# Scatters queued behind the next masks, ranks in another buffer, even rows on VectorE, and a tail in another order

## The chip, the cores and the metric

The kernel runs on one core of one Trainium2 chip. The metric is the device time of one launch in microseconds. Each core has TensorE (matmuls, PE in the profile; PEld are its weight loads), VectorE (DVE), ScalarE (ACT), GpSimd (POOL) and SyncE (SP, which here only issues DMAs).

## The reference

Three layers, one behind the other, over 4 x 768 = 3072 tokens of 8 heads x 48 = 384 values, all in float32.

```
state = alpha_t * state + k_t v_t^T ;  y_t = q_t state           # linear attention with decay
e = argmax(x @ w_gate) ; p = softmax(...)[e] ; s = sigmoid(x @ w_output_gate)[e]
x2 = p * s * (relu(x @ w1[e]) @ w2[e])                            # top-1 of 8 experts, F = 1024
out = relu(x2 @ w_in)**2 @ w_out                                  # dense, F = 2048
```

## The kernel before

**Attention loop.** The tokens are cut into 24 chunks of 128 (six to a batch entry). All matrix work of a chunk is done on TensorE with several chunks in flight: iteration i of the loop (line 783) does scores(i+1), scaled(i+2) (k and q turned, and multiplied with the decay), rows(i-1) and logits(i-1) (attention output back to one row per token, and the gate logits), decay(i+3) (two scans on VectorE), khat(i+1), outputs(i) and update(i+1) (the state). The order of these calls is the order in which each engine gets its instructions; each engine works its queue in that order and waits by semaphores.

- scores (328): 16 matmul instructions into two PSUM tiles `sc`; ScalarE copies them to `m`, and GpSimd cuts out the causal half of each with an affine_select (341), the "masks". For the last two chunks VectorE does both at once (346).
- outputs (389) writes PSUM tile `y`, and ScalarE copies it to `yt` (407). rows (418) multiplies `yt` into PSUM tile `fx`; ScalarE copies 384 columns of it to `xn` (433), and logits (435) sums the other columns on VectorE.
- The PSUM tiles `y`, `fx` and `ku` have one buffer each, `sc` two.

**Routing.** Chunks form groups of 6, 6, 6, 3, 1, 1, 1 (GROUPS). When a group's logits are there, route (448) puts some ten small VectorE operations (softmax, argmax, one-hot) on an agenda, and every call of pulse(n) in the loop issues n of them. One iteration later, settle (351) issues ranks (496), small matmuls that count for each token how many earlier tokens chose its expert, and place (519), which reads them (`rp`, 524); nine further small steps (placed, 527) give the index `idx` and the gate `g`. Then move(n) (566) scales up to n rows of the group by their gate (even chunks on ScalarE, 572, odd ones on VectorE, 570) and at once scatters each to the DRAM buffer `xs`, sorted by expert, with an indirect DMA that GpSimd issues (scatter, 142: a small memset and the DMA). `pace` is 1 for iterations below 18 and 3 from there; move stands at three places of an iteration.

**Early experts.** The expert with the most tokens of groups 0 to 2 is picked, and at the end of iteration 20 gather_early (680) issues two DMAs that read its first 256 tokens back from `xs` into `gx`; they wait for all scatters before them.

**Tail** (815 to 863). After the loop: the last outputs; turn_early (690) turns the gathered tokens on TensorE (`tx`), ScalarE and VectorE split them in a high and a low half (696, 697: lambdas that run(steps) calls); parts(3) (184) splits the weights of unit 3 (ScalarE cast 186, VectorE subtraction 187); the groups of one chunk are routed by route_one (577), placed by place_one (629: rank matmuls, then `rp` 634 and `idx` 636 on VectorE) and sent by send (639). psum (486) says which buffer a rank tile uses. Then up1 (719) and down1 (737) begin the experts, three matmuls for each product (`three`, 1353: high and low halves).

**Experts and dense layer** (995 to 1134). 64 units of expert weights, then 16 of the dense layer over 6 blocks of 512 tokens, a stream of matmuls beside which weights are loaded and split.

Of the kernel before, what the change touches and what calls it, by code (L numbers as in the profile page):

```python
# [27 lines left out]
def moe_block_kernel(ctx: ExitStack, tc: tile.TileContext, q, k, v, alpha, w_gate, w_ogate,  # L28
# [39 lines left out]
    with tc.manual_schedule():  # L68
# [115 lines left out]
        def parts(n, engine=nc.gpsimd):  # L184
            w, raw = unit_tile(n), raws.pop(n)
            nc.scalar.copy(w[:, 0::2, :], raw)  # L186
            engine.tensor_tensor(out=w[:, 1::2, :], in0=raw, in1=w[:, 0::2, :].bitcast(F32),  # L187
                                 op=ALU.subtract)
# [86 lines left out]
        def pulse(n=2):  # L275

            while agenda and n:
                if next(agenda[0], None) is None:
                    agenda.pop(0)
                else:  # L280
                    n -= 1

        def decay(i, mid=None):
            if i >= NCH:
                return
            ps = turned("al", i)
            al = al_t[i % 2]
            nc.scalar.copy(al[:, 0:PQ].rearrange("p (r t) -> p r t", r=NP)[:, :, 1:],
                           ps[:, :, 1:])
            s = a3.tile([P, 2, PQ], F32, tag="sp", name="sp", bufs=4)  # L290
            suf, pre = s[:, 0, :], s[:, 1, :]
            nc.vector.tensor_tensor_scan(suf[:, ::-1], al[:, 1:PQ + 1][:, ::-1],
                                         ends.rearrange("p c t -> p (c t)")[:, ::-1],
                                         initial=0.0, op0=ALU.mult, op1=ALU.add)
            pe = a3.tile([P, NP], F32, tag="pend", name="pend", bufs=4)
            nc.vector.tensor_tensor(out=pe, in0=ps[:, :, 0], in1=suf[:, 0:PQ:P], op=ALU.mult)
            pend[i] = pe
            pulse()
            sp[i] = s
            if mid:  # L300
                mid()
            d = d1_t[i % 2]
            nc.vector.reciprocal(d[:, 0:PQ:P], suf[:, 0:PQ:P])
            nc.vector.tensor_tensor_scan(pre, al[:, 0:PQ], d, initial=0.0, op0=ALU.mult,
                                         op1=ALU.add)
            pulse()

        def scaled(i, nms="kq"):
            if i >= NCH:
                return  # L310
            s = sp[i]
            for nm in nms:
                j, dst = (0, kh) if nm == "k" else (1, qh)
                ps = turned(nm, i)
                t = a3.tile([P, NP, P], F32, tag=nm + "h", name=nm + "h")
                nc.vector.tensor_tensor(out=t, in0=ps,
                                        in1=s[:, j, :].rearrange("p (r t) -> p r t", r=NP),
                                        op=ALU.mult)
                dst[i] = t
                pulse()  # L320
# [7 lines left out]
        def scores(i):  # L328
            if i >= NCH:
                return  # L330
            ps = [p_sc.tile([P, NP, P], F32, tag="sc", name="sc") for _ in range(2)]
            for pr in range(NP):
                for a in range(2):
                    r = slice(64 * a, 64 * a + D)
                    nc.tensor.matmul(ps[a][:, pr, :], kh[i][r, pr, :], qh[i][r, pr, :],  # L335
                                     start=True, stop=True)
            for a in range(2):
                m = ms_p.tile([P, NP, P], F32, tag="m", name="m")
                if i < NCH - 2:
                    nc.scalar.copy(m, ps[a])  # L340
                    nc.gpsimd.affine_select(out=m, in_=m, pattern=[[0, NP], [1, P]],
                                            compare_op=ALU.is_ge, fill=0.0, base=0,
                                            channel_multiplier=-1)
                else:

                    nc.vector.tensor_tensor(out=m, in0=ps[a],
                                            in1=mask.unsqueeze(1).to_broadcast([P, NP, P]),
                                            op=ALU.mult)
                msk[i, a] = m

        def settle(groups):
            for gi in groups:
                place(gi, ranks(gi))
# [14 lines left out]
        def update(i):  # L368
            if not has_next(i):
                return  # L370
            t = khn.pop(i)
            vt = slot("v", i)
            ps = p_1.tile([P, NP, D], F32, tag="ku", name="u")
            for pr in range(NP):
                for a in range(2):
                    nc.tensor.matmul(ps[64 * a:64 * a + 64, pr, :], t[:, pr, 64 * a:64 * a + 64],  # L376
                                     vt[:, 2 * pr + a, 0:D], start=True, stop=True)
            s = state[i % 3][:, :, 0:D]
            pb = pend[i + 1].unsqueeze(2).to_broadcast([P, NP, D])
            if i % NC == 0:  # L380
                nc.vector.tensor_tensor(out=s, in0=ps, in1=pb, op=ALU.mult)
            else:
                nc.vector.tensor_tensor(out=s, in0=ps, in1=st[i], op=ALU.add)
                pulse()
                nc.vector.tensor_tensor(out=s, in0=s, in1=pb, op=ALU.mult)
            st[i + 1] = s
            pulse()
# [98 lines left out]
        def psum(n):  # L486
            if late_ps:
                late_ps["n"] += 1
                return late_ps["t"][:, late_ps["n"]:late_ps["n"] + 1, :]
            else:  # L490
                t = p_1.tile([P, BLK], F32, tag="ku" if n == 3 else "fx", name="rk")
            return t[:, 0:n * E].rearrange("p (c e) -> p c e", e=E)

        late_ps = {}
# [71 lines left out]
        def move(n):  # L566
            for i, g in moving[:n]:
                x = xn.pop(i)
                if i % 2:
                    nc.vector.tensor_scalar(x, x, g, None, op0=ALU.mult)  # L570
                else:
                    nc.scalar.activation(x, x, AF.Copy, scale=g)
                scatter("xs", xs, idx[:, i:i + 1], x)
                sent.add(i)
            del moving[:n]

        def route_one(gi):

# [60 lines left out]
        def send(i):  # L639
            x = xn.pop(i)  # L640
            nc.scalar.activation(x, x, AF.Copy, scale=routing[group[i][0]][2])
            scatter("xs", xs, idx[:, i:i + 1], x)
# [47 lines left out]
        def turn_early(kk):  # L690
            ps = p_tr.tile([P, BLK], F32, tag="tr", name="tx")[:, 0:EARLY]
            for i, t in enumerate(early["g"]):
                nc.tensor.transpose(ps[:, i * P:(i + 1) * P], t[:, kk * P:(kk + 1) * P], ident)
            xsp[0, kk] = hi, lo = [early[nm][:, kk, :] for nm in ("xh", "xl")]
            c = first_part
            nc.scalar.copy(hi[:, c], ps)
            return lambda: nc.vector.tensor_tensor(out=lo[:, c], in0=ps, in1=hi[:, c].bitcast(F32),
                                                   op=ALU.subtract)
# [84 lines left out]
        for i in range(NCH - 2):  # L783
            pace = 1 if i < gstart[PICK] else 3
            scores(i + 1)
            scaled(i + 2)
            if i:
                rows(i - 1)
                logits(i - 1)
            decay(i + 3)  # L790
            khat(i + 1)
            move(pace)
            if i == NCH - 3:
                finish()
            outputs(i)
            if i < NCH - 3:
                check(i)
            move(pace)
            update(i + 1)

            settle([gi for gi in routing if gi in waited])
            waited.update(routing)
            pulse()
            move(pace)
            for e in (range(E - 2, E) if i == E - 1 else range(i - 1, i) if 0 < i < E - 1 else ()):
                clear(e)
            if i == gstart[PICK - 1] + 2:
                pick()
            if 0 <= i - gstart[PICK - 1] - 2 < NRA + 2:
                fetch(i - gstart[PICK - 1] - 2)  # L810
            if i == NCH - 4:
                gather_early()
            if i in ready:
                parts(ready.index(i), nc.vector)
# [11 lines left out]
        logits(i - 2)  # L826
        finish()
        outputs(i)
        steps = [turn_early(kk) for kk in range(NK)]
        parts(3, nc.vector)  # L830
        one = group[i - 2][0]
        place_one(one)
        send(i - 2)
        run(steps)
        rows(i - 1)
        logits(i - 1)
        rows(i)
        pulse(4)
        logits(i)
# [579 lines left out]
```

## Time and profile before

| | |
|---|---|
| median of 3 timed runs | 818.91 us (817.11 to 820.15) |
| the profiled execution | 811.78 us, of which the span is 810.0 us |
| mean granted TensorE clock | 0.995 |
| PE busy | 793.0 us (98%), 5389 matmul instructions |
| PEld busy | 725.9 us (90%) |
| DVE busy | 500.5 us (62%) |
| ACT busy | 374.4 us (46%) |
| POOL busy | 230.5 us (28%) |

The profile is of one execution. Busy time counts an engine's instructions; matmuls are pipelined, so 98% is not 98% of what TensorE could do. A wait is idle time in front of an instruction, with the engine and line whose end released it; where an instruction waits for several, the last by the profile is named. The attention loop with its tail takes up to about 167 us, the rest is the experts and the dense layer.

### The profile page before, as it was taken

Reading aid. Unit: us, or ns where it says so; the run is one execution under the profiler, and the core shown is the slowest. Engines: PE = TensorE matmul, PEld = TensorE weight load, DVE = VectorE, ACT = ScalarE, POOL = GpSimd, SP = SyncE. Lnnn points to the kernel's source line nnn. Section 1 sums busy time; section 2 is a strip of 40 time slices with the busy share of each in tenths; the row PEclk is TensorE's granted clock in tenths of the full one; section 3 lists DMA queues with packets and bytes.
Section 4 is the critical chain, followed back from the end, with each engine's and each line's share of the span. In section 5 each row is a group of like instructions: output and inputs, shape, how many; then the busy total and the mean of one; then the engine's idle time right before and its main releaser. Section 6 shows DMA issues by size and latency. Waiting matters only on the chain.

```text
span 810.0 us, 14449 instructions
## 1 busy us (share of the span) xinstructions
PE 793.0 (98%) x5389; PEld 725.9 (90%) x5389; DVE 500.5 (62%) x954; ACT 374.4 (46%) x689; POOL 230.5 (28%) x275
## 2 busy tenths in 40 slices
PE   9999999899999999999999999999999999999995
PEld 6898889799999999999998999999999999999995
DVE  8778799867567966987787786443333433333331
ACT  4676667554554565556443443433232333333231
POOL 4123543323546766777400000220001002002002
PEclk9999999999999999999999999999999999999998
DMA  9999969344545665885312010110001001001001
GB/s 138 177 205 212 201 152 215 96 131 155 169 150 143 181 177 147 194 177 172 64 40 58 23 58 21 40 39 1 1 1 40 0 1 40 1 0 40 1 1 42
DMA packets 153861, 74.99 MB, mean 93 GB/s; under 512 B 105406, under 2 KB 149430, under 8 KB 153782
## 3 DMA queue, kind: packets, MB, share of 16 engines
q1 hardware_dynamic: 149878, 64.52, 36.0%
q0 software_dynamic: 3904, 9.47, 3.4%
q8 instruction: 44, 0.72, 0.4%
q14 instruction: 35, 0.29, 0.1%
HBM read 61.76 MB, written 12.20 MB: 91 GB/s over the span
## 4 chain that ended last, share of the span: by engine, by line
PE 60%; issue 31%; DVE 4%; POOL 3%; DMA 1%; ACT 1%; POOLq 0%; SPq 0%; DVEq 0%; ACTq 0%
PE ha L1356 7%; PE ha L1357 7%; PE ha L1358 7%; PE acc L1356 7%; PE acc L1357 7%; PE acc L1358 7%; PE tr L268 3%; PE sc L335 2%; PE y L402 2%; PE fx L423 2%; POOL out_dram L145 2%; PE y L398 2%; PE tx L918 1%; PE khp L363 1%; PE u L376 1%
## 5 line engine op out<-in xcount | busy, mean ns | idle before, releaser
L1357 PE MATMUL ha<-xl,w 128*128 128x512 f32 (+7 forms) x456 | 172.8, 379 | 0.0
L1358 PE MATMUL ha<-xh,w 128*128 128x512 f32 (+7 forms) x456 | 172.5, 378 | 0.0
L1356 PE MATMUL ha<-xh,w 128*128 128x512 f32 (+7 forms) x456 | 172.2, 378 | 0.0
L946 DVE SCALAR_TENSOR_TENSOR r<-ha,r 128x512 f32<-128x512 f32 x96 | 66.2, 690 | 139.8 <-ACT r L945 139.7
L187 POOL TENSOR_TENSOR w<-raw,w 128x768 fp32r<-128x768 f32 x58 | 110.6, 1907 | 81.2 <-ACT w L186 67.0
L145 POOL DMA_INDIRECT out_dram<-o,ids x24 | 23.1, 963 | 379.2 <-DVE o L974 355.4
L945 ACT ACTIVATE r<-ha 128x512 f32<-128x512 f32 x96 | 57.2, 596 | 157.6 <-PE ha L1358 157.3
L1358 PE MATMUL acc<-w,hl 128*128 128x384 f32 x380 | 128.1, 337 | 0.0
L1357 PE MATMUL acc<-w,hh 128*128 128x384 f32 x380 | 127.5, 336 | 0.0
L1356 PE MATMUL acc<-w,hh 128*128 128x384 f32 x380 | 127.5, 335 | 0.0
L956 DVE TENSOR_TENSOR hl<-r,hh 128x512 fp32r<-128x512 f32 x95 | 65.8, 692 | 65.3 <-PE acc L1358 44.7
L955 ACT CAST hh<-r 128x512 fp32r<-128x512 f32 x95 | 59.0, 621 | 88.0 <-DVE r L946 88.0
L1358 PEld LDWEIGHTS ha<-xh,w 128*128 128x128 f32 x456 | 85.8, 188 | 12.9
L1356 PEld LDWEIGHTS ha<-xh,w 128*128 128x128 f32 x456 | 85.8, 188 | 9.9
L1357 PEld LDWEIGHTS ha<-xl,w 128*128 128x128 f32 x456 | 85.8, 188 | 9.8 <-DVE xl L930 0.3
L186 ACT CAST w<-raw 128x768 fp32r<-128x768 f32 x64 | 53.5, 836 | 57.2 <-PE acc L1358 48.3
L1357 PEld LDWEIGHTS acc<-w,hh 128*128 128x128 f32 x380 | 71.4, 188 | 4.4
L1356 PEld LDWEIGHTS acc<-w,hh 128*128 128x128 f32 x380 | 71.4, 188 | 4.0
L1358 PEld LDWEIGHTS acc<-w,hl 128*128 128x128 f32 x380 | 71.4, 188 | 0.0
L1356 PE MATMUL acc<-hh,w 128*128 128x456 f32 (+7 forms) x174 | 61.3, 352 | 0.0
L1357 PE MATMUL acc<-hl,w 128*128 128x456 f32 (+7 forms) x174 | 60.8, 349 | 0.0
L1358 PE MATMUL acc<-hh,w 128*128 128x456 f32 (+7 forms) x174 | 60.7, 349 | 0.0
(223 smaller groups left out, 1296.1 us busy)
## 6 DMA issues: line engine op xcount, KB each, us to landing
raw<-in_moe_w_dram SPq DMA_DIRECT2D x128, 192.0 KB, 3.5
bits<-in_moe_w_in_dram SPq DMA_DIRECT2D x16, 384.0 KB, 4.2
bits<-in_moe_w_out_dram SPq DMA_DIRECT2D x16, 384.0 KB, 6.1
nat_al<-in_alpha_dram SPq DMA_DIRECT2D x24, 192.0 KB, 5.2
nat_k<-in_k_dram SPq DMA_DIRECT2D x24, 192.0 KB, 5.6
nat_q<-in_q_dram SPq DMA_DIRECT2D x24, 192.0 KB, 5.1
nat_v<-in_v_dram SPq DMA_DIRECT2D x24, 192.0 KB, 4.3
gx<-xs SPq DMA_DIRECT2D x22, 192.0 KB, 5.0
```

The source lines that it names most:

```text
L145: ins = nc.gpsimd.indirect_dma_start(out=dst[:, :], out_offset=bass.IndirectOffsetOnAxis(ap=ix, axis=0), in_=src, in_offset=None)
L186: nc.scalar.copy(w[:, 0::2, :], raw)
L187: engine.tensor_tensor(out=w[:, 1::2, :], in0=raw, in1=w[:, 0::2, :].bitcast(F32), op=ALU.subtract)
L268: nc.tensor.transpose(ps[:, pr, :], src[:, pr, :], ident)
L335: nc.tensor.matmul(ps[a][:, pr, :], kh[i][r, pr, :], qh[i][r, pr, :], start=True, stop=True)
L945: nc.scalar.activation(r, ps, AF.Relu)
L946: nc.vector.scalar_tensor_tensor(out=r, in0=ps, scalar=0.0, in1=r, op0=ALU.max, op1=ALU.mult)
L955: nc.scalar.copy(hh, r)
L956: nc.vector.tensor_tensor(out=hl, in0=r, in1=hh.bitcast(F32), op=ALU.subtract)
L1356: nc.tensor.matmul(ps, st[0], mv[0], start=start, stop=False)
L1357: nc.tensor.matmul(ps, st[0], mv[1], start=False, stop=False)
L1358: nc.tensor.matmul(ps, st[1], mv[0], start=False, stop=stop)
```

## The change

- pulse in decay, between the two scans, issues 3 steps in place of 2.
- psum gives a rank tile of six chunks the `y` buffer in place of `fx`, and one of a single chunk a buffer of `sc` (the later single ones have their own, late_ps); one of three keeps `ku`.
- move scales even rows on VectorE and odd rows on ScalarE, and only notes them; flush issues the scatters. In the loop flush stands behind scores(i+1) in every iteration, and from iteration 18 on behind each move as well.
- settle and the set `waited` move from behind update(i+1) to behind scores of the next iteration, with a pulse if a group was settled.
- From iteration 18 on update stands ahead of the second move.
- In the tail place_one comes first, then parts(3), send and rows(i-1); only then turn_early, logits(i-1), one step of routing and the low halves, and rows(i).

```diff
@@ decay
-            pulse()
+            pulse(3)
@@ psum
-                t = p_1.tile([P, BLK], F32, tag="ku" if n == 3 else "fx", name="rk")
+                t = (p_sc.tile([P, BLK], F32, tag="sc", name="rk") if n == 1 else
+                     p_1.tile([P, BLK], F32, tag="ku" if n == 3 else "y", name="rk"))
@@ move
                 if i % 2:
+                    nc.scalar.activation(x, x, AF.Copy, scale=g)
+                else:
                     nc.vector.tensor_scalar(x, x, g, None, op0=ALU.mult)
-                else:
-                    nc.scalar.activation(x, x, AF.Copy, scale=g)
+                scaled_rows.append((i, x))
+            del moving[:n]
+
+        scaled_rows = []
+
+        def flush():
+            for i, x in scaled_rows:
                 scatter("xs", xs, idx[:, i:i + 1], x)
                 sent.add(i)
-            del moving[:n]
+            scaled_rows.clear()
@@ the loop
             scores(i + 1)
+
+            flush()
+            ready_now = [gi for gi in routing if gi in waited]
+            settle(ready_now)
+            waited.update(routing)
+            if ready_now:
+                pulse()
             scaled(i + 2)
             ...
             khat(i + 1)
-            move(pace)
+            move(1)
+            if pace > 1:
+                flush()
             ...
-            move(pace)
-            update(i + 1)
-
-            settle([gi for gi in routing if gi in waited])
-            waited.update(routing)
+            if pace > 1:
+                update(i + 1)
+                move(pace)
+                flush()
+            else:
+                move(pace)
+                update(i + 1)
             pulse()
             move(pace)
+            if pace > 1:
+                flush()
@@ the tail
         outputs(i)
-        steps = [turn_early(kk) for kk in range(NK)]
-        parts(3, nc.vector)
         one = group[i - 2][0]
         place_one(one)
+        parts(3, nc.vector)
         send(i - 2)
+        rows(i - 1)
+        steps = [turn_early(kk) for kk in range(NK)]
+        logits(i - 1)
+        pulse(1)
         run(steps)
-        rows(i - 1)
-        logits(i - 1)
         rows(i)
```

## Rows read from the trace of the kernel before

**Rows 1.** Waits of TensorE, 0 to 360 us: total us, times, longest us.

```profile
PE fx L423 <- DVE rp L634: 2.4, 1, 2.4
PE tx L693 <- DMA gx<-xs: 1.5, 2, 0.8
```

**Rows 2.** Chain of waits, 31 to 38 us: start us, us, what.

```profile
31.17 1.02 PE y L402 x16
...
34.76 0.88 PE fx L423 x8
...
37.53 1.02 PE y L402 x16
```

**Rows 3.** Stretches: length, busy us (instructions) by engine, PEclk, DMA share, GB/s.

```profile
164.00:165.00 1.00, 1.00 (x6) 1.00 (x6) 0.73 (x3) 0.00 (x0) 0.81 (x3) 0.50 0.52 192
...
167.00:168.00 1.00, 1.00 (x10) 1.00 (x10) 0.77 (x7) 0.51 (x3) 0.00 (x0) 0.98 0.05 18
```

**Rows 4.** Timeline, 75 to 83 us: start, us, instruction, [idle before <-releaser].

```profile
75.54 1.48 POOL L145 DMA_INDIRECT xs<-xn,idx  x1 [9.62 <-ACT khn L365]
...
77.70 1.06 ACT L340 COPY m<-sc 128x512 f32<-128x512 f32 x2
...
79.83 2.16 POOL L341 TENSOR_SCALAR_AFFINE_SELECT m<-m 128x512 f32<-128x512 f32 x2
...
80.54 0.19 PEld L402 LDWEIGHTS y<-m,nat_v 128*64 128x64 f32 x2 [0.30 <-POOL m L341]
...
82.05 0.85 PEld L402 LDWEIGHTS y<-m,nat_v 128*64 128x64 f32 x14 [1.32 <-POOL apart L144]
```

**Rows 5.** Timeline, 140 to 142 us, around the rank of group 2.

```profile
140.33 0.47 PEld L268 LDWEIGHTS tr<-ident,nat_q 128*128 128x128 f32 x4
...
140.89 0.20 DVE L524 TENSOR_TENSOR rp<-rk,onehot 128x48 f32<-128x48 f32 x1
...
141.21 0.97 PEld L423 LDWEIGHTS fx<-wx,yt 128*128 128x128 f32 x8 [0.41 <-ACT m L340]
```

**Rows 6.** Timeline, 146 to 158 us: rows of group 2, their scatters, the gather.

```profile
146.60 1.12 ACT L572 ACTIVATE xn<-xn,g 128x384 f32<-128x384 f32 x2 [2.65 <-DVE g L560]
...
147.49 1.03 POOL L145 DMA_INDIRECT xs<-xn,idx  x1 [5.40 <-ACT xn L572]
...
148.24 0.97 PEld L423 LDWEIGHTS fx<-wx,yt 128*128 128x128 f32 x8 [0.64 <-ACT yt L407]
...
153.88 1.23 POOL L145 DMA_INDIRECT xs<-xn,idx  x1 [0.19 <-issue]
...
156.75 1.68 SPq L685 DMA_DIRECT2D gx<-xs  x2
```

**Rows 7.** Timeline, 157 to 171 us: the tail and the first expert units.

```profile
157.56 1.09 PE L402 MATMUL y<-m,nat_v 128*64 128x128 f32 x16
...
158.57 0.17 DVE L608 SCALAR_TENSOR_TENSOR onehot<-ei,em 128x8 bf16<-128x8 f32 x1
...
160.45 0.77 PE L693 MATMUL tx<-ident,gx 128*128 128x128 f32 x5 [0.65 <-DMA gx<-xs]
...
161.61 0.85 ACT L186 CAST w<-raw 128x768 fp32r<-128x768 f32 x1
...
163.37 0.15 DVE L634 SCALAR_TENSOR_TENSOR rp<-rk,onehot 128x8 f32<-128x8 f32 x1
...
163.69 3.61 PE L423 MATMUL fx<-wx,yt 128*128 128x112 f32 x16 [2.44 <-DVE rp L634]
...
167.07 0.37 PE L1356 MATMUL ha<-early,w 128*128 128x256 f32 x1
...
170.59 0.37 PE L1356 MATMUL acc<-early,w 128*128 128x256 f32 x1
```

**Rows 8.** A scan beside masks (timeline, 87 us), and all such scans (by line).

```profile
87.27 2.14 DVE L292 TENSOR_TENSOR_SCAN sp<-al,ends 128x512 f32<-128x512 f32 x1 [0.36 <-ACT al L288]
...
L292 DVE TENSOR_TENSOR_SCAN sp<-al,ends 128x512 f32<-128x512 f32 x24 | 31.1, 1295 | 4.7 <-ACT al L288 4.7
```

## The prediction

> **What bounds the kernel now.** I first asked which engine the end hangs on, then where that engine stands still. By the table above TensorE is busy for 98% of the span and VectorE for 62%. The list of waits by TensorE then says how little idle time there is to win: from 0 to 360 us its two largest waits are 2.4 and 1.5 us [rows 1], and after 360 us the same list is empty. So from the experts on, every microsecond by which TensorE starts earlier reaches the end, and whatever does not move TensorE is worth nothing.
>
> The chain of waits gives the loop's pace: `y` of one chunk starts at 31.17 and of the next at 37.53, 6.36 us of matmul back to back [rows 2]. The loop is at TensorE's own pace; what can be won there are single stalls. In the tail after the loop it is different. The last `y` ends at 157.56 + 1.09 = 158.65, the first expert matmul starts at 167.07 [rows 7]: 8.42 us, in which stand two `rows` of 0.88 us each [rows 2], six transposes (about 0.8 us, five took 0.77) and four short rank matmuls (about 0.2 us): 2.75 us. The other 5.67 us are waits, and a clock: `rows` x16 takes 3.38 us from 163.69 to 167.07 instead of 1.76 [rows 7], because the granted clock is 0.50 (1.2 GHz) from 164 to 165 and full again (0.98 in the row) by 167 to 168 [rows 3]. It fell after 2.4 us without a matmul [rows 1]. It cost 3.38 - 1.76 = 1.62 us.
>
> **The change part by part.** I count only the time of TensorE; durations are of the profiled execution (811.78 us, span 810.0).
>
> *Scatters behind the next masks.* In the loop GpSimd takes scatters ahead of the next chunk's masks. The first scatter sits until 75.54, the masks for chunk 10 start only at 79.83, and TensorE stands 0.30 and 1.32 us in the middle of `y` [rows 4]. In the new order scores(i+1) queues its two masks first and the three scatters of the iteration before follow. ScalarE's two copies for these masks are done at 77.70 + 1.06 = 78.76, and a pair of masks takes at most the 2.16 us of this one, with the first of them begun a copy earlier: they end by 80.3, before `y` asks (80.54). Gain 1.62 us. Added behind the masks: three scatters at about 1.28 us from start to start (the six from 147.49 to 153.88, [rows 6]), 3.8 us inside a period of 6.36: the masks after next are not late. Bound: the same stall at another chunk, once for each of the two groups moved this way, 0 to 3.2 us; I take 0, since 3.8 + 2.2 us of masks fit the period.
>
> *Ranks behind the scores, in the outputs' buffer.* A rank matmul shared the `fx` buffer, so the next `rows` waited until VectorE had read it: the transposes' weights end at 140.33 + 0.47 = 140.80, `rp` runs at 140.89, `rows` starts at 141.21 [rows 5], 0.41 us. (The bracket names ScalarE, but the buffer is freed by `rp`, which ends just before.) Three groups of six chunks: 0.41 twice and 0.28 once, 1.1 us. In the `y` buffer the next user is outputs(i), behind `rows` (0.88) and eight transposes, almost 2 us after `rp`. The rank matmuls themselves stay, now behind the scores; `rp` doesn't become later, as VectorE is busy with the state in front of it until 140.89 anyway.
>
> *Gates ahead of the second scan, even rows by VectorE.* Before, the first row of a group (even) is ScalarE's, and it stands at the head of ScalarE's queue waiting for the gate: 2.65 us idle until 146.60, and behind it `yt`, without which `rows` cannot start: 0.64 us [rows 6]. With three steps in the pulse the gate's reciprocal comes 1.2 us sooner, ahead of the scan, and the row that needs it first is VectorE's own. ScalarE goes straight to `yt`. Of this kind I find 0.15 and 0.17 us in groups 0 and 1, and the 0.64 in group 2. The last I don't count: behind it VectorE runs without a pause until the routing of chunk 21 (onehot 158.57, [rows 7]), so TensorE would only wait there. VectorE scales three rows in six as before, so its sum is the same; the extra small operation ahead of the scan (0.16 to 0.6 us) delays only what the next iteration reads. Loop in all: 1.62 + 1.10 + 0.32 = **3.0 us**; bounds 0 (stalls only move) and 3.7 (with the 0.64).
>
> *Scatters of group 2.* The early gather waits for all six: the last starts at 153.88, the gather is issued at 156.75 [rows 6] and its second part reaches TensorE at 160.45 [rows 7]. New: row 12 follows the second scan on VectorE (about 147.0, scatter near 147.25 instead of 147.49), row 13 is ScalarE's, behind `yt` and the check of chunk 20 (about 147.8), and from there the six run at the same 1.28 us. So the second part comes at 160.2, 0.25 us earlier. Bound: if each odd row waits for ScalarE's queue, up to 1.5 us later.
>
> *Tail reordered.* Before, TensorE waited for the gather (1.5 us in two pieces), then for `rp` at 163.37, which stood on VectorE behind a weight part that needs ScalarE's half of it, made at 161.61 behind the early copies [rows 1, 7]; all because rank and `rows` shared a buffer. New, in the clock of the old trace: onehot is ready at 158.74, ranks 158.9 to 159.1, rows(22) needs neither gather nor `rp`: 159.1 to 160.0; gather there at 160.2, transposes to 160.75; rows(23) to 161.65. ScalarE beside it: yt(23) after 158.65, then its half of the weight part (0.85), send and xn (I put 1.2 for both, each being half to three quarters of that cast's width), so the three early copies start near 161.2 and end near 162.1; VectorE's three subtractions follow one copy behind, each slice in time for its matmuls or 0.2 us late. So the first expert matmul starts at 161.65 instead of 167.07: 5.4 us, with no long empty stretch, so I take the clock as staying up.
> What is late next: down1(0) (170.59 before, [rows 7]) needs VectorE's part of the first unit, which stands behind both routings. Before, they fitted between the end of `rows` (167.1) and 170.59 with that part behind them, 3.5 us. Now they start when logits(22) is read (about 160.9), give way to the three subtractions (about 1.1 us), and the first unit's part is there near 160.9 + 1.1 + 3.5 = 165.5, or 166.1 with xn and send in ScalarE's way. TensorE would want it 161.65 + (170.59 - 167.07) = 165.2: a wait of 0.3 to 0.9, taken as 0.7. Tail: 5.4 - 0.7 = **4.7 us**; bounds 2.0 (gather 1.5 later in place of 0.25 earlier, and another 1 us for the routings) and 5.7 (all of it).
>
> **Sum.** 3.0 + 4.7 = 7.7 us: the profiled execution of 811.8 becomes 804.1. The timed runs lie 7.1 us above the profiled one (818.91); the stalls are in the kernel in either case, so I take the same 7.7 off: 811.2.
>
> **A rule weighed.** One scan took 2.14 us beside a pair of masks on GpSimd; the mean of all 24 is 1.295 [rows 8]. In the new order three scatters, one behind the other, run beside the scans of the same iteration.
> The Trainium skill ("SBUF — State Buffer", section "Who interferes with whom") says that VectorE and GpSimd share a pair of ports: an operation of VectorE with two SBUF inputs, or in a two-port mode, and a GpSimd operation that reads SBUF shut each other out for a whole instruction. By that rule the even rows (a tensor_scalar from SBUF to SBUF) join in as well. The 2.14 agrees with it. It speaks against the change, so its result is a rival below.
>
> **Rivals.**
> 1. *The gather is the bound.* ScalarE's rows 13, 15, 17 stand behind the check. With the gather 1.5 us later than before TensorE waits 2 us in front of the transposes and the clock falls again (1.6 us): 7.7 - 1.8 - 1.6 = 4.3, 814.6. For: ScalarE's queue is the one thing that got longer ahead of row 13. Against: POOL needs a row only every 1.28 us. Chance 0.12.
> 2. *The loop gives nothing* (stalls move to the next masks or the next `yt`): the tail's 4.7 alone, 814.2. Chance 0.10.
> 3. *Scans and scatters shut each other out.* Two bursts for each of groups 0 and 1, two scans each, 0.85 us a scan (2.14 - 1.295): 6.8 us if VectorE sets the pace there, which leaves 0.9: 818.0. Against: seen once in full in the old trace, and the period is TensorE's. Chance 0.06.
> 4. *Slower: the clock.* The new tail still has four short waits (onehot, gather, early copies, down1). If they together take the clock down near 159 and it stays down through the first units, until the short waits end (about 12 us of full-speed work), that work takes twice as long: +12 - 7.7 = +4.3, 823.2. It decides from 7.7 us of such work on. For: it fell in this very place. Against: it fell only after 2.4 us with nothing, and came back within 3.4 us of work [rows 3, 7]. Chance 0.04.
> 5. *It doesn't do what it says*: the ranks' new buffers or the row order bring a wait of the old size; 817 to 820. Chance 0.05.
>
> My forecast has the remaining 0.63. About 0.5% (4.1 us) is what a measurement of this kernel can tell from no change. Faster by more than that: the forecast less a little (0.59), half of rival 1, most of rival 2, together 0.74; slower: rival 4 and some of 5, 0.06; the rest 0.20. Range: the best case is 3.7 + 5.7 = 9.4 us (809.5) and the timed runs spread by 1.5 us either way; downwards it takes in rivals 1 and 2 with the same spread: 808.5 to 816.5.
>
> **What would show it.** Right: no wait of `y` for GpSimd near 80 us; `rows` following the transposes without a gap in the three rank iterations; ScalarE not idle before its scaled rows; rows(22) ahead of the transposes of the gathered rows, a granted clock of 1.00 throughout; the first expert matmul some 8 us earlier than 167.07 (3.0 + 5.4), down1(0) 7.7 earlier than 170.59. Wrong: waits for the gather of over 1.5 us, a clock of 0.5 near 160, or new waits of TensorE between 75 and 130 us.

## The result, and the profile after

The changed kernel takes 829.16 us (median of 4 runs, 825.16 to 830.89) against 818.66 of the kernel before (817.11 to 820.15, with a fourth run beside the three above): ratio 1.0125, 95% interval 1.0093 to 1.0158. It is slower by 10.5 us, where I had forecast 7.7 us faster (811.2, range 808.5 to 816.5). The profiled execution took 830.89 us, span 829.2, mean granted clock 0.98 in place of 0.995.

The three largest waits of TensorE from 0 to 360 us in the changed kernel (total us, times, longest us). The two large ones of [rows 1] are gone, and these stand in their place (`khn` is ScalarE's copy in khat, which update on TensorE reads):

```profile
PE u L376 <- ACT khn L365: 6.2, 3, 2.2
PE sc L335 <- issue: 2.2, 6, 0.5
PE ha L1378 <- DVE early L705: 1.8, 1, 1.8
```

The timeline of the changed kernel (start us, us, instruction, idle before), in five pieces: a routing iteration; the masks and scatters that answer to [rows 4]; the rank of group 2 [rows 5]; its scatters [rows 6]; the tail [rows 7]:

```profile
54.88 1.09 PE L402 MATMUL y<-m,nat_v 128*64 128x128 f32 x16
...
55.21 1.23 DVE L292 TENSOR_TENSOR_SCAN sp<-al,ends 128x512 f32<-128x512 f32 x1 [0.36 <-ACT al L288]
...
56.84 0.21 DVE L464 TENSOR_TENSOR df<-lg,mx 128x48 f32<-128x48 f32 x1
...
57.08 0.24 ACT L475 ACTIVATE ex<-df 128x48 f32<-128x48 f32 x1 [1.91 <-DVE df L464]
...
57.23 0.57 ACT L365 COPY khn<-khp 128x512 f32<-128x512 f32 x1
...
57.85 0.67 PE L376 MATMUL u<-nat_v,khn 128*64 128x48 f32 x16 [1.88 <-ACT khn L365]
...
66.56 1.10 PE L402 MATMUL y<-m,nat_v 128*64 128x128 f32 x16
...
85.57 1.22 POOL L341 TENSOR_SCALAR_AFFINE_SELECT m<-m 128x512 f32<-128x512 f32 x2 [3.18 <-ACT m L340]
...
86.48 0.85 PEld L402 LDWEIGHTS y<-m,nat_v 128*64 128x64 f32 x16 [0.17 <-issue]
...
86.98 1.90 POOL L145 DMA_INDIRECT xs<-xn,idx  x1 [0.15 <-issue]
...
155.26 0.21 DVE L525 TENSOR_TENSOR rp<-rk,onehot 128x48 f32<-128x48 f32 x1
...
155.88 0.97 PEld L423 LDWEIGHTS fx<-wx,yt 128*128 128x128 f32 x8
...
161.59 1.62 ACT L571 ACTIVATE xn<-xn,g 128x384 f32<-128x384 f32 x3
...
161.87 0.97 POOL L145 DMA_INDIRECT xs<-xn,idx  x1 [4.91 <-DVE st L383]
...
170.55 0.59 ACT L407 COPY yt<-y 128x512 f32<-128x512 f32 x1 [4.35 <-remote]
...
178.58 1.09 PE L402 MATMUL y<-m,nat_v 128*64 128x128 f32 x16
...
182.51 0.93 ACT L704 CAST early<-tx 128x256 fp32r<-128x256 f32 x3
...
182.99 1.08 DVE L705 TENSOR_TENSOR early<-tx,early 128x256 fp32r<-128x256 f32 x3
...
184.12 0.39 PE L1378 MATMUL ha<-early,w 128*128 128x256 f32 x1 [1.79 <-DVE early L705]
...
189.16 0.37 PE L1378 MATMUL acc<-early,w 128*128 128x256 f32 x1
```

The first piece is the loss. ScalarE's Exp of the routing (`ex`) now stands ahead of `khn` in ScalarE's queue. It waits for VectorE's `df`, a routing step that stands behind the first of the two scans; `khn` waits with it, and so does `update` on TensorE. From one `y` to the next it is 11.68 us (54.88 to 66.56) where [rows 2] show 6.36. Once per group of six: 11.68, 10.46 and 11.88 us where the kernel before has 6.36, 6.53 and 6.36, together 14.8 us.

The wait is only 6.2 of it; the rest is the clock. Stretches of the changed kernel (length; busy us and instructions of PE, PEld, DVE, ACT, POOL; PEclk; DMA share; GB/s), around the first of these waits:

```profile
57.00:58.00 1.00, 0.15 (x4) 0.15 (x6) 0.93 (x4) 0.92 (x3) 0.00 (x0) 1.00 0.55 105
59.00:60.00 1.00, 1.00 (x14) 1.00 (x12) 0.90 (x5) 0.34 (x2) 0.00 (x0) 0.50 1.03 218
64.00:65.00 1.00, 1.00 (x7) 1.00 (x6) 0.22 (x1) 0.48 (x1) 0.00 (x0) 0.50 1.41 180
66.00:67.00 1.00, 1.00 (x20) 0.83 (x18) 0.90 (x2) 0.29 (x1) 0.00 (x0) 1.00 1.18 244
```

About 2 us nearly without a matmul, and TensorE works at 1.2 GHz (0.50) until 65 us. (14.8 - 6.2) / 3 = 2.9 us a time are left for the clock, more than the wait itself. The trace bears that out: the granted clock is 0.50 from 58.4 to 65.3, from 102.8 to 106.2 and from 143.8 to 150.6 us, 17.1 us in all, and work at half the clock loses half of that, 8.5 us.

### The profile page after: what moved, and what is told of

It is laid out like the page before. It is cut to its first block, busy times and chain, and to the rows that moved or that the text cites. A ratio compares the mean times of both kernels' runs of the same rounds, so it can differ in the third digit from the quotient of the medians.

```text
span 829.2 us, 14444 instructions
## 1 busy us (share of the span) xinstructions
PE 804.4 (97%) x5389; PEld 735.5 (89%) x5389; DVE 505.1 (61%) x954; ACT 374.0 (45%) x689; POOL 227.6 (27%) x275
## 4 chain that ended last, share of the span: by engine, by line
PE 59%; issue 30%; DVE 3%; POOL 2%; ACT 2%; DMA 1%; SPq 0%; POOLq 0%; DVEq 0%; ACTq 0%
PE ha L1378 7%; PE ha L1380 7%; PE ha L1379 7%; PE acc L1379 7%; PE acc L1378 7%; PE acc L1380 7%; PE tr L268 3%; PE sc L335 3%; PE fx L423 2%; PE y L402 2%; PE y L398 2%; POOL out_dram L145 2%; PE tx L940 1%; PE u L376 1%; PE khp L363 1%
## 5 line engine op out<-in xcount | busy, mean ns | idle before, releaser
L186 ACT CAST w<-raw 128x768 fp32r<-128x768 f32 x64 | 53.5, 836 | 58.4 <-PE acc L1380 44.2
```

## Experiments

**Is it the third step of the pulse?** e1: the changed kernel with the old pulse. e2: the old kernel with the new pulse. e3: the changed kernel, the Exp issued with the group's last step.

```diff
 e1 (changed kernel)          e2 (kernel before)
-            pulse(3)        -            pulse()
+            pulse()         +            pulse(3)
 e3 (changed kernel, route)
-            nc.scalar.activation(ex, df, AF.Exp)
             ...
             count(gi)
+            nc.scalar.activation(ex, df, AF.Exp)
```

> The changed kernel with two steps again in the pulse between the scans. Theory: with three steps there, the routing of a group of six reaches its fifth step inside decay, and that step puts an Exp on ScalarE ahead of the copy khn; the Exp waits for VectorE, the copy waits behind it, TensorE's state matmuls wait 2 us for the copy and the clock falls. The three iterations concerned take 11.68, 10.46 and 11.88 us instead of 6.36, 6.53 and 6.36: 14.8 us. Without them: 829.2 - 14.8 + 1 (the gates late again) = 815.4 (813 to 818), no low clock near 58, 103 and 144 us. Rival: the loss lies in the last iterations (six scatters in a row, the stop of all engines at 166 to 170 us, the clock in the tail): 823 or more.

> The kernel before with three steps in that pulse and nothing else. Theory: the same three stalls, 818.7 + 14 = 832 (826 to 835), with TensorE waiting for khn about 2 us at each of three places. Rival: the pulse is harmless, 817 to 820.

> The changed kernel with its pulse of three, but route issues its Exp only with its last step. Theory (it is the Exp in ScalarE's queue and not VectorE's extra step ahead of the scan): the stalls go, and the gates stay early: 814.4 (812 to 817), 1 us better than with two steps. Rival a (VectorE's extra operation delays the scan): as the changed kernel, 826 to 831. Rival b (the last iterations): 823 or more.

e1: 818.49 us, ratio to the kernel before 0.9989 (0.9971 to 1.0007). e2: 827.23, 1.0101 (1.0062 to 1.0139): the pulse alone makes the old kernel 8.6 us slower. e3: 817.65, 0.998 (0.9963 to 0.9998): with `pulse(3)` kept and only the Exp later, 11.5 us come back. So it is the place of the Exp in ScalarE's queue and nothing else about the pulse (e1 and e3 do not differ clear of noise). The timeline of e3 at the same iteration has `khn` 2.2 us earlier, no wait, and the Exp behind everything urgent:

```profile
55.06 0.59 ACT L365 COPY khn<-khp 128x512 f32<-128x512 f32 x1
...
55.80 0.62 PE L376 MATMUL u<-nat_v,khn 128*64 128x48 f32 x16
...
57.60 0.23 ACT L483 ACTIVATE ex<-df 128x48 f32<-128x48 f32 x1
```

But e1 and e3 were expected near 815; the rest of the change brought 0.1 to 1.0 us, not 7.7. The experiments below take that rest apart.

**The tail alone** (e4: the kernel before with the new order of the tail, and the rank of a single chunk in `sc`).

```diff
+        place_one(one)
+        parts(3, nc.vector)
+        send(i - 2)
+        rows(i - 1)
         steps = [turn_early(kk) for kk in range(NK)]
-        parts(3, nc.vector)
-        place_one(one)
-        send(i - 2)
+        logits(i - 1)
+        pulse(1)
         run(steps)
-        rows(i - 1)
-        logits(i - 1)
```

> The kernel before with the tail in the new order and the single chunks' rank in a buffer of the scores, and nothing else. My step in the prediction: 4.7 us less, 814 (812 to 816). From the changed kernel's trace, where the first expert matmul still waits 1.8 us for VectorE's half and starts 5.5 us behind the last y instead of 8.4: at least 2.9 us less, 816. Rival (the short waits bring the clock down): 818 or more.

816.52, 0.998 (0.9958 to 1.0002): 2.1 us between the medians, not 4.7, and not clear of noise, since the interval reaches 1. Its trace has 10.82 us between the `y` of chunks 21 and 22, and those of e1 to e3 have 10.9 to 11.6, where the profile that the prediction rests on has 4.74. So that profile itself was in question.

**The kernel before, profiled once more** (e5, unchanged).

> The kernel before, unchanged, looked at again: its first profiled execution was 811.78 us, 7 us below the median of its timed runs, and had 4.74 us between the y of chunks 21 and 22, while every changed kernel so far has 10.6 to 11.6 us there: TensorE, VectorE and ScalarE come nearly to a stop for 2 to 4 us beside the last of the six scatters of group 2, and the granted clock is 0.5 behind it. Theory S (the stop is what the kernel before usually has too, and the first profile was a rare execution without it): the time is 816 to 820 us, 10 us or more between these two y, a granted clock of 0.5 from about 155 us for 6 us or more, and the first expert matmul at 172 to 175 us in place of 167.07. Rival (the stop came with each edit): a span near 810 to 812 us again with 4.7 us between these y, and then the timed runs are longer for a reason outside the profiled stretch.

817.11 us (one run), span 815.4. The timeline of e5: a pair of masks that answers to [rows 4], the stretch around chunk 21, and the tail:

```profile
79.88 1.23 POOL L341 TENSOR_SCALAR_AFFINE_SELECT m<-m 128x512 f32<-128x512 f32 x2
...
147.49 1.03 POOL L145 DMA_INDIRECT xs<-xn,idx  x1 [5.40 <-ACT xn L572]
...
150.78 1.09 PE L402 MATMUL y<-m,nat_v 128*64 128x128 f32 x16
...
152.62 0.96 POOL L145 DMA_INDIRECT xs<-xn,idx  x1 [0.19 <-issue]
...
153.16 0.28 PE L376 MATMUL u<-nat_v,khn 128*64 128x48 f32 x2 [0.84 <-issue]
...
153.87 0.27 PE L335 MATMUL sc<-qh,kh 48*128 48x128 f32 x1 [0.44 <-issue]
...
153.89 0.96 POOL L145 DMA_INDIRECT xs<-xn,idx  x1 [0.19 <-issue]
...
156.00 1.66 PE L335 MATMUL sc<-qh,kh 48*128 48x128 f32 x12 [0.91 <-issue]
...
156.16 0.59 ACT L407 COPY yt<-y 128x512 f32<-128x512 f32 x1 [4.62 <-remote]
...
156.27 0.36 DVE L383 TENSOR_TENSOR st<-u,st 128x192 f32<-128x192 f32 x1 [3.75 <-remote]
...
161.56 1.76 PE L402 MATMUL y<-m,nat_v 128*64 128x128 f32 x14
...
165.37 1.10 PE L402 MATMUL y<-m,nat_v 128*64 128x128 f32 x16
...
169.93 2.01 PE L423 MATMUL fx<-wx,yt 128*128 128x112 f32 x16 [2.63 <-DVE rp L634]
...
171.71 0.36 PE L1356 MATMUL ha<-early,w 128*128 128x256 f32 x1
```

TensorE issues a matmul only every 0.7 us, VectorE does nothing for 3.75 us and ScalarE for 4.62, while GpSimd goes on with its scatters; the stretches of e5 show the clock fall behind it:

```profile
153.00:154.00 1.00, 0.40 (x3) 0.32 (x2) 0.00 (x0) 0.00 (x0) 0.81 (x3) 1.00 0.37 137
...
160.00:161.00 1.00, 1.00 (x13) 1.00 (x11) 0.91 (x8) 0.36 (x2) 0.00 (x0) 0.50 0.00 0
```

I call this the stop. The kernel before has it too; the execution whose rows stand ahead of the prediction was without it. Eleven profiled executions of all these kernels send the six scatters of group 2 in a row, 1.3 to 1.6 us apart: ten have the stop, with 10.3 to 11.6 us between these two `y`, and only the one of [rows 6] is without. All timed runs of the kernel before, in all sessions, lie between 816.0 and 822.6 us; none came near 811.78. From the end of the last `y` to the first expert matmul it is 171.71 - 166.47 = 5.24 us here, against 8.42 in the execution of [rows 7]: the stop makes the loop late, and the gather is there by the time the tail wants it.

**What brings the stop?** e7 (changed kernel with e3's Exp) and e10 (kernel before) spread group 2's scatters over two iterations, with the gather an iteration later.

```diff
 e10 (e7: 1, 1, 1 in both iterations)
+            PLACES = {i: (3, 3, 3), NCH - 4: (1, 1, 1), NCH - 3: (0, 1, 2)}
-            move(pace)
+            move(PLACES[i][0] if pace > 1 else 1)      # likewise at the other two places
-            if i == NCH - 4:
+            if i == NCH - 3:
                 gather_early()
```

> The changed kernel with the Exp of a group issued with its last routing step, and with the six scatters of group 2 spread over two iterations, one at each of the three places instead of one, three and two, and the gather an iteration later. Theory S3 (the stop between chunks 21 and 22 comes from six scatters in a row 1.3 us apart): no stretch in which TensorE issues one instruction in 0.7 us, 21 to 22 takes 4.7 to 6 us, no granted clock of 0.5 before 165 us; the gather comes 5 to 7 us later and TensorE waits for it 3 to 5 us, with a low clock behind that, so that the time is 814 to 819. Rival (the stop has its cause in something else at this place: the pick, the wait of the queue that loads, the end of the loop): 21 to 22 stays at 10 us or more, and with the later gather the time is 819 to 823.

> The kernel before with one edit: the six scatters of group 2 go out three in iteration 20 and three in iteration 21 (none at its first place), and the gather is issued at the end of iteration 21. Theory S3 (four or more scatters in a row, 1.3 us apart, bring the stop of TensorE, VectorE and ScalarE; three don't, as groups 0 and 1 of the kernel before show): 4.7 to 5.5 us between the y of chunks 21 and 22 in place of 10.78, no granted clock of 0.5 near 155 us, 6 us won there; the gather comes some 4 us later against the loop and TensorE waits for it up to 3 us; the time is 812 to 816. Rival (it is the place, not the number of scatters in a row): 10 us again between these y, and with the later gather 818 to 822.

e7: 812.82, 0.9931 (0.9907 to 0.9956), better than expected, since the gather was nearly in time (a wait of 0.3 us); four scatters in a row leave a half stop (8.17 us between these `y`, not 4.7 to 6). e10: 814.46, 0.9945 (0.9924 to 0.9967), 4.7 us from this one edit. The timeline of e10, three scatters, 2.2 us, three more:

```profile
150.12 0.96 POOL L145 DMA_INDIRECT xs<-xn,idx  x1 [0.19 <-issue]
...
150.28 1.09 PE L402 MATMUL y<-m,nat_v 128*64 128x128 f32 x16
...
152.32 0.96 POOL L145 DMA_INDIRECT xs<-xn,idx  x1 [1.13 <-DVE xn L570]
...
155.30 1.09 PE L402 MATMUL y<-m,nat_v 128*64 128x128 f32 x16
...
163.94 3.73 PE L423 MATMUL fx<-wx,yt 128*128 128x112 f32 x16 [2.44 <-DVE rp L634]
```

From `y` to `y` 5.02 us: the stop is gone, and the tail's wait and low clock of [rows 7] are back. So the run of scatters has to do with it, and it isn't the place alone. The edit also issues the gather an iteration later, which no run does by itself; but e7 and e14, with the gather just as late and four scatters 1.27 us apart, keep a part of the stop (8.17 and 7.47 us). Why the engines stop is not shown: the execution of [rows 6] had the same six scatters, 1.28 us apart, and no stop.

**The other parts of the change.** e8: e3 with the rows scaled as before. e11: the kernel before with the rows the new way. e6: e3 with each scatter issued as its row is scaled. e13: the kernel before with the noted scatters, settle behind the scores, the rank of six chunks in `y` and, from iteration 18 on, update ahead of the second move.

```diff
 e11 (e8: the reverse)
                 if i % 2:
-                    nc.vector.tensor_scalar(x, x, g, None, op0=ALU.mult)
-                else:
                     nc.scalar.activation(x, x, AF.Copy, scale=g)
+                else:
+                    nc.vector.tensor_scalar(x, x, g, None, op0=ALU.mult)
 e6
-                scaled_rows.append((i, x))
+                scatter("xs", xs, idx[:, i:i + 1], x)
+                sent.add(i)
 e13: flush, settle, psum's "y" and update's place from the change, nothing else of it
```

> The changed kernel with the Exp of a group issued with its last routing step, and with the even rows scaled by ScalarE and the odd ones by VectorE as in the kernel before; scatters still noted and flushed behind the next masks. Theory S2 (the bursts of scatters hold up group 1, whoever scales): 13 to 17 stay within 0.5 us of 8.07, 6.60, 7.48 and 5.60 us, the time is 817 to 819. Rival (two rows in one iteration on VectorE are what is in the way, ahead of the key of the pick and of the state): 13 to 14 falls to about 7.0 and 15 to 16 to about 6, and the time is 814 to 816.

> The kernel before with one edit: even rows are scaled by VectorE and odd rows by ScalarE. Theory R (the change of the rows costs time by itself: in the changed kernel, taking it back was worth 817.65 - 813.83 = 3.8 us): the time is 820 to 823, with the loss between chunks 13 and 17, where TensorE waits for the key of the pick and for yt. Rival (it costs only beside the noted and flushed scatters): within 1 us of the kernel before, 817.5 to 819.5. My forecast had put a gain of 0.32 us on the rows and gates together.

> The changed kernel with the Exp of a group issued with its last routing step (as in the run before, 817.65 us) and besides with each scatter issued as soon as its row is scaled, not noted and flushed behind the next masks. Theory S2 (the deferred scatters, three in a row, hold GpSimd and the engines beside it in group 1, which cost about 5 us from chunk 13 to 17: 8.07, 6.60, 7.48 and 5.60 us from y to y where the kernel before had 7.07, 6.66, 5.93 and 5.92): these become 6.5 to 7.1, 6.7, 5.9, 5.9, and the time 814 to 816. The stall of y behind a scatter in group 0, which the deferral was to remove, comes back (1.5 us near chunk 10). Rival (the changed order of rows and of settle is what costs it there): 13 to 17 stay as they were within 0.5 us, and the time is 817 to 819.

> The kernel before with the noted and flushed scatters, settle behind the scores and the rank of six chunks in the outputs' buffer; rows, pulse and tail as before. Theory (these two edits do in the loop what the forecast said, 2.7 us, of which most runs keep what the stop between chunks 21 and 22 doesn't take back): the iterations 7 to 8, 13 to 14 and 19 to 20, 6.93, 7.06 and 7.07 us in the kernel before, become 6.5 each, the y of chunk 21 starts 1 to 2 us ahead of 150.8, and the time is 816 to 818. Rival (bursts of flushed scatters give it back between chunks 13 and 17): 818 to 820.

e8: 813.83, 0.9944 (0.9924 to 0.9963): 3.8 us less than e3 between the medians, 2.9 by the ratios to the kernel before, whose intervals just meet. e11: 817.91, 0.9993 (0.9976 to 1.001): the new rows cost the old kernel nothing, so my theory that they cost by themselves fell. e6: 816.59, 0.9982 (0.9966 to 0.9998), the same ratio as e3's. The traces show a trade behind it. In e3 the 8.07, 6.60, 7.48 and 5.60 us belong to chunks 14 to 18 (the expectations of e6 and e8 count them one chunk too low); in e6 these are 7.70, 5.93, 5.92 and 5.34, 2.9 us less. From chunk 9 to 11 it takes 14.27 us in place of 12.14, 2.1 more: the waits of `y` for scatter and masks near chunk 10 are back, 1.1 and 0.8 us. So in these executions the noted scatters cost 2.9 us in group 1 and won 2.1 in group 0. e13: 816.55, 0.998 (0.9968 to 0.9992), 1.8 us; the iterations named there became 6.53 us as expected, and chunk 14 to 15 gave a part back: 7.48 us in place of 6.66 in e5, with a wait of 0.8 for `key`, VectorE's small operation with which the early expert is picked and whose PSUM tile has the buffer of `rows`.

**Together** (e9, e12): the changed kernel with e3's Exp, the old rows, group 2 spread, the pick's matmul in a buffer of the transposes (`tr`), and the early copies ahead of unit 3's cast and of send. Then e14 and e15: e12 with the new rows, and with scatters at once.

```diff
 e12 (e9: NCH - 3: (0, 1, 2)), besides the edits of e3, e8, e10
+            PLACES = {i: (3, 3, 3), NCH - 4: (1, 1, 1), NCH - 3: (1, 1, 1)}
-  p_1.tile([P, E], F32, tag="fx", name="cps")
+  p_tr.tile([P, NP, P], F32, tag="tr", name="cps")[:, 0, 0:E]
         place_one(one)
-        parts(3, nc.vector)
-        send(i - 2)
         rows(i - 1)
         steps = [turn_early(kk) for kk in range(NK)]
         logits(i - 1)
-        pulse(1)
         run(steps)
+        parts(3, nc.vector)
+        send(i - 2)
         rows(i)
+        pulse(1)
```

> The changed kernel with what the runs so far speak for: the Exp of a group with its last routing step, rows scaled as before (even ScalarE, odd VectorE), the six scatters of group 2 three and three over two iterations with the gather at the end of the second, the pick's small matmul in a transposes' buffer instead of that of rows, and in the tail the early copies ahead of the cast of unit 3 and of send. Theory: no stop between chunks 21 and 22 (about 5 us won against 813.83), no wait of rows for the pick's key (0.6), the early low halves in time (1 to 1.9 less), a wait for the gather of 1 to 3 us: 807 to 811. Rival (the stop comes with three and three as well, or the later gather gives all of it back): 813 to 816.

> The same with the six scatters of group 2 at one row for each of the three places of two iterations, as in the run that had them spread (there four came in a row and two 2.5 us later, a half stop of 8.17 us was left between chunks 21 and 22 with a granted clock of 0.5 for 3.4 us, and the gather was in time). Theory: 4 in a row bring a part of the stop again, about 3 us, but the gather is 1.3 us earlier: 808 to 812, slower than three and three by 0.5 to 3 us if the gather is hidden, and faster if it is what TensorE waits for in the tail.

> The fastest version (808.33) with even rows on VectorE and odd ones on ScalarE. Theory K (the rows' price in the changed kernel was the pick: VectorE's key stood behind two scaled rows while rows waited for its buffer, 1.4 us, and the next yt behind that, 1.3 us; here the pick has another buffer): 808 to 809.5. Rival (rows that VectorE scales beside the flushed scatters hold up the loop by themselves): 811 to 813, with 7 us or more in the iterations from chunk 13 to 16.

> The fastest version (808.33) with each scatter issued as soon as its row is scaled. Theory (the flush is worth what the forecast gave it, 1.62 us, through the wait of y for the masks in group 0): 809.5 to 811, with 1.3 to 1.9 us of waits for the masks or for the scatter ahead of them near 80 us. Rival (without the stop nothing hangs on the flush, or it costs as much elsewhere): 807.5 to 809.

e9: 809.13, 0.9887 (0.9865 to 0.9909). e12: 808.33, 0.9873 (0.9853 to 0.9894), faster than both kernels, by 10.8 us than the one before in the same session. e9 waits 2.1 us for the gather, e12 0.7, but their intervals overlap. The largest waits of TensorE in e12 from 0 to 200 us, beside one of 1.1 us before the first chunk: none for `khn`, and the gather nearly hidden:

```profile
PE rk L502 <- DVE rp L642: 1.1, 1, 1.1
PE rk L502 <- DVE onehot L616: 1.1, 1, 1.1
PE tx L701 <- DMA gx<-xs: 0.7, 1, 0.7
```

e14: 810.47, 0.9917 (0.9895 to 0.994). e15: 809.97, 0.9912 (0.988 to 0.9944). e14's interval begins where e12's ends, so that its rows cost something, 2.1 us between the medians, 3.6 by the ratios; e15's overlaps e12's, and that the scatters at once cost 1.6 us is not settled. The timeline of e14 shows one place where its rows cost something, at a burst of three noted scatters 1.27 us apart: a matmul group stretched from 1.16 to 1.64 us and a late `yt`, the stop in small. That iteration, chunk 15 to 16, takes 7.08 us against 5.92 in e12, whose three scatters there come 2.2 and 1.6 us apart; the one before it takes 7.08 against 6.48:

```profile
112.23 0.99 POOL L145 DMA_INDIRECT xs<-xn,idx  x1 [0.19 <-issue]
...
113.20 0.20 PE L376 MATMUL u<-nat_v,khn 128*64 128x48 f32 x1 [0.46 <-issue]
...
113.33 1.64 PE L335 MATMUL sc<-qh,kh 48*128 48x128 f32 x16
...
114.11 0.58 ACT L407 COPY yt<-y 128x512 f32<-128x512 f32 x1 [2.65 <-PE u L376]
```

`key` is no longer in front of `rows` (its wait is 0.4 us), so theory K explains at most a part of the rows' price; the two iterations above 7 us are what its rival expected, though the time lies between both.

## Why the prediction was wrong

**The step that failed** is in the part on the gates: "the extra small operation ahead of the scan (0.16 to 0.6 us) delays only what the next iteration reads". I counted VectorE's operation and not what the agenda issues behind it. With three steps ahead of the second scan the fifth step falls into the pulse behind it, ahead of `khat`, and that step is ScalarE's Exp. ScalarE then stood 1.91 us for `df`, and `khn`, queued behind, set TensorE: 14.8 us in the loop of the profiled execution. Taking it out alone (e3) is worth 829.2 - 816.1 = 13.1 us between the profiled spans and 11.5 between the medians. None of my rivals had it. Rival 5 foresaw "a wait of the old size"; rival 4 was right that short waits take the clock down, but placed them in the tail alone. (The range was also added up a little short: 9.4 us less and 1.5 of spread is 808.0, not 808.5. Nothing hangs on it.)

**The second wrong step** is the sentence "the stalls are in the kernel in either case". The 7.1 us between the profiled execution and the timed runs was for the most part not an offset but a stall inside the stretch I was arguing about. e5 is 5.3 us longer than that execution: the stop puts the end of its last `y` 7.8 us later (166.47 against 158.65), and the shorter tail gives 3.2 back. With the stop the tail has 5.24 us in place of 8.42, and the gather isn't what it waits for. By my own count 2.75 of it are work, so that no order of the tail could win more than 2.5 us there, where I had put 5.4.

**By part.**
- *Scatters behind the next masks* and *ranks in the outputs' buffer*: the mechanism was right. `y` at 86.48 has no wait for GpSimd where [rows 4] had 0.30 and 1.32; behind `rp` and the transposes `rows` starts at 155.88 without a bracket, where [rows 5] had 0.41. The size was 1.8 us (e13), not 2.72: the noted scatters of group 1 came in bursts beside the pick. And the 1.62 was that of one execution: in e5, with the same kernel, the pair of masks at 79.88 takes 1.23 us in place of 2.16, the two waits of `y` are 0.22 and 0.39, and chunk 10 to 11 takes 6.49 us in place of 7.42.
- *Even rows by VectorE*: ScalarE has no wait before its rows any more (161.59, against 2.65 in [rows 6]). In place of 0.32 won, 3.8 us were lost beside the other edits (e3 to e8), nothing without them (e11). `key` behind two rows is a part of it. For the rest the trace of e14 points at noted scatters that come closer together; that is not shown by a run of its own.
- *Scatters of group 2*: the six ran 1.27 us apart (161.87 to 168.21), as I had put (1.28), but the stop lies on them. TensorE waits for the gather nowhere, so rival 1 has no part in the loss.
- *Tail*: the order did what I said, and the early copies start at 182.51, 2.8 us behind the last `y` (178.58 + 1.09), where I had 2.55 (161.2 - 158.65). What failed is "each slice in time for its matmuls or 0.2 us late": the first expert matmul starts at 184.12, not behind the first of VectorE's three subtractions but behind the last (182.99 + 1.08 = 184.07; in e4 170.79 and 170.84). TensorE waits 1.79 us for it, with the clock at 0.50 behind it, so that down1 comes 5.04 us after up1 in place of 3.52. From the end of the last `y` to down1 it is 9.49 us here, 8.77 in e5 and 7.35 in e4: alone the new tail won 1.4 us in the profiled executions and 2.1 between the medians, in place of 4.7, and in the changed kernel nothing.
- *The rule weighed*: the by-line row of the changed kernel puts the first scan at 1246 ns, against 1295 in [rows 8], so the scans on the whole did not get longer beside the bursts; rival 3 has no part in the loss. One scan still took 1.80 us, at 91.70, beside a pair of masks of 2.16.

```profile
L292 DVE TENSOR_TENSOR_SCAN sp<-al,ends 128x512 f32<-128x512 f32 x24 | 29.9, 1246 | 8.0 <-ACT al L288 7.6 <-issue 0.4
```

The rule of the Trainium skill ("SBUF — State Buffer", "Who interferes with whom") speaks of either side being shut out; here a scatter beside a scan stretched too, to 1.90 us (86.98), which nothing in the loop waited for.

The sum by the runs, from 818.66: -1.8 (e13), -2.1 (e4), +3.8 (rows, e8), +11.5 (Exp, e3) gives 830.1; measured 829.16. The last two terms are differences between neighbouring kernels up to the changed one, so they close by themselves; what the sum tests is that the first two, -3.9, come near to e8's 813.83 - 818.38 = -4.6.

## What to carry to other kernels

Where an agenda issues work for several engines, follow each step to the engine whose queue it enters and ask what is queued behind it there; one tiny activation that waited 2 us held up a whole pipeline here, and the clock then charged 2.9 us more. If the profiled execution lies outside the timed runs, find out where the difference is before sizing anything from that profile.

## What the runs showed of the hardware

- The granted clock went to 0.50 after waits of 1.9 to 2.2 us in the loop and stayed there to 65 us for the first of them; the tail's 1.79 us did the same.
- In ten of eleven profiled executions with six indirect scatters in a row, 1.3 to 1.6 us apart, TensorE, VectorE and ScalarE came nearly to a stop: VectorE idle for 2.8 to 4.0 us, ScalarE for 3.5 to 4.7, TensorE's instructions in e5 0.7 us apart with no wait that the trace names. The eleventh, that of [rows 6], had none.
- Four scatters 1.27 us apart left a part of it (8.17 us from `y` to `y` in e7, 7.47 in e14), four 1.27 to 1.64 us apart little (5.73 in e12, 5.76 in e15), and three and three with 2.2 us between them none (5.02 in e10). In small it came beside three as well: ScalarE stood 2.65 us ahead of `yt` in e14. What decides it is open.
